# The second feed-forward's partial outputs: from sums in SBUF by DVE to copies by ACT and accumulating DMAs into DRAM

## The chip, the cores and the metric

One core of one Trainium2 chip runs the whole program. The metric is the device time of one execution in microseconds (us); the kernel before takes 995.15 us, the median of 3 runs (994.6 to 995.23).

## The reference

An attention with a memory term makes `x` of 2304 tokens by 512. Two feed-forwards follow, each with a hidden width of 2048:

```python
x = attn_out.transpose(0, 2, 1, 3).reshape(2304, 512)
h = x @ w_in                       # 512 -> 2048
x = (h * tanh(softplus(h))) @ w_out    # first feed-forward, 2048 -> 512
h = x @ w_in2
return (h * sigmoid(h)) @ w_out2       # second feed-forward
```

Inputs and output are float32.

## The kernel before, in words

The attention runs in the first 250 us. The two feed-forwards (`ph` 0 and 1) follow in 32 visits. The hidden width is cut into `NG` = 4 groups (`g`), the tokens into 4 blocks (`tp`) of 512, 640, 512 and 640 tokens. One visit `v` computes one group for one block, and the list says in which order the visits stand:

```python
VISITS = [(ph, g, tp) for ph in range(2) for g in range(NG)
          for tp in (range(4) if (g + ph) % 2 == 0 else range(3, -1, -1))]
```

So the blocks of the second feed-forward are passed as 3, 2, 1, 0, then 0, 1, 2, 3, and so on; where a group ends, the next one begins with the same block (visits 19 and 20, 23 and 24, 27 and 28). Each visit has two halves of seven products (`product`, a scheme that saves multiplications; tiles `psX`, `psW`, `psY` in PSUM, lines 962 to 964), whose results ACT and DVE turn into the hidden values `g` (lines 991 to 1003). Then `out_part` (L1030) multiplies `g` by the second weights into a PSUM tile `acc`, of which there are three. In the second feed-forward such a tile is 128 tokens by 512 outputs, and a visit has 4 or 5 of them (`d`). Every `acc` takes 12 matmuls, six from either half of the visit, and is then drained (`drain`).

A group gives only a part of the output, so four drains add up to one output tile. Before the change the sum stands in `xT` in SBUF: the first group's `acc` is copied there by ACT (L1049), the three later ones are added to it by DVE (L1051). After the last group `store` (L1056) sends the tile to the output in DRAM from SP's queue. The last tile of a block of 640 tokens (`d` = 4) lies in `xT` as four pieces of 128 elements for each partition, not as one of 512.

The order on every engine is worked out ahead of the build by a planner (`Steps.plan`): each step has an engine (P, A, D, G, S for TensorE, ACT, DVE, POOL, SP), an assumed duration, the steps that it waits for, a due time and the buffers that it holds, and a table `SHIFT` moves due times. Engines run their lists in order. SP's queue also carries the loads of the weights (L755, L759), the spills of the split inputs of a block (L940) and their reloads (L944). POOL works in the attention and for the first weights, and has nothing to do after 223 us.

Of the kernel before, what the change touches and what calls it, by code (L numbers as in the profile page):

```python
# [22 lines left out]
ALU = mybir.AluOpType  # L23
# [9 lines left out]
def latency(a, b):  # L33
    return LAT.get(a + b, 0.25)


class Steps:
# [35 lines left out]
    def plan(self):  # L73
# [15 lines left out]
        for k in reversed(topo):  # L89
            e, d, _, _, due = ops[k]  # L90
# [31 lines left out]
        while done < len(ops):  # L122
            while soon and soon[0][0] <= now + 1e-9:
                _, n, k = heapq.heappop(soon)
                heapq.heappush(ready[ops[k][0]], (late[k], n, k))
            while rel and rel[0][0] <= now + 1e-9:
                used[heapq.heappop(rel)[1]] -= 1
            moved = False
            for e in engs:
                if free[e] > now + 1e-9 or not ready[e]:  # L130
                    continue
                put_back = []
                while ready[e]:
                    it = heapq.heappop(ready[e])
                    k = it[2]
                    need = [h for h in self.takes.get(k, []) if h not in held]
                    count = {}
                    for h in need:
                        count[h[0]] = count.get(h[0], 0) + 1
                    ok = all(used[r] + c <= self.cap[r] for r, c in count.items())  # L140
                    ok = ok and all(h not in self.order_of or nexts[h[0]][0] == h for h in need)
                    if not ok:
                        put_back.append(it)
                        if len(put_back) > 40:
                            break
                        continue
                    for h in need:
                        held.add(h)
                        used[h[0]] += 1
                        if h in self.order_of:  # L150
                            nexts[h[0]].pop(0)
                    d = ops[k][1]
                    if e == "P" and self.mode.get(k, 0) != mode:
                        mode = self.mode.get(k, 0)
                        d += 0.15
                    if k in self.cols:
                        cycles, count = self.cols[k]
                        if passed.get(int(now / TICK) - 1, 0.0) < BUSY:
                            d = max(d, cycles / 1200.0)
                        t = now  # L160
                        while t < now + d - 1e-9:
                            q = int(t / TICK + 1e-9)
                            b = min(now + d, (q + 1) * TICK)
                            passed[q] = passed.get(q, 0.0) + count * (b - t) / d
                            t = b
                    self.start[k] = now
                    order.append(k)
                    free[e] = now + d
                    done += 1
                    for u in users.get(k, []):  # L170
                        left[u] -= 1
                        at[u] = max(at[u], now + d + self.lag[k] + latency(e, ops[u][0]))
                        if left[u] == 0:
                            heapq.heappush(soon, (at[u], num[u], u))
                    for h in back.get(k, []):
                        due_back[h] -= 1
                        if due_back[h] == 0:
                            heapq.heappush(rel, (now + d + 0.2, h[0]))
                    moved = True
                    break  # L180
                for it in put_back:
                    heapq.heappush(ready[e], it)
            if not moved:
                t = [x for x in free.values() if x > now + 1e-9]
                if soon:
                    t.append(soon[0][0])
                if rel:
                    t.append(rel[0][0])
                t = [x for x in t if x > now + 1e-9]
                if not t:  # L190
                    raise RuntimeError(f"stuck at {now}: " + str({e: sorted(v)[:3] for e, v in ready.items()}))
                now = min(t)
# [11 lines left out]
B, H, S, D = 4, 8, 576, 64  # L204
# [134 lines left out]
class Attn:  # L339
# [329 lines left out]
    def register(self, m):  # L669
# [6 lines left out]
        for p in range(B * NP):  # L676
# [22 lines left out]
KC = DM // P  # L699
NF = FF // P  # L700
NG = 4
# [6 lines left out]
VISITS = [(ph, g, tp) for ph in range(2) for g in range(NG)  # L708
          for tp in (range(4) if (g + ph) % 2 == 0 else range(3, -1, -1))]
# [14 lines left out]
def cuts(v):  # L724
    return [DM] if VISITS[v][0] or TBS[VISITS[v][2]] * 2 == DM else [TBS[VISITS[v][2]]]


def ps2(n):
    return 0.126 + n / 960


def sb1(n):
    return 0.093 + n / 1200
# [154 lines left out]
class Moe:  # L888
# [154 lines left out]
    def drain(self, v, d):  # L1043
        nc = self.nc
        ph, g, tp = VISITS[v]
        part, acc = self.part(v, d), self.acc.pop((v, d))
        acc = acc[:, :cuts(v)[0]] if ph == 0 else acc if d < KC else acc.rearrange("p (c n) -> p c n", c=KC)
        if g == 0:
            nc.scalar.copy(part, acc)  # L1049
        else:  # L1050
            nc.vector.tensor_tensor(part, acc, part, op=ALU.add)  # L1051

    def store(self, v, d):
        r = START[VISITS[v][2]] + d * P
        to = self.out[r:r + P, :]
        self.nc.sync.dma_start(to if d < KC else to.rearrange("p (c n) -> p c n", c=KC), self.part(v, d))  # L1056

    def register(self, m, base, ends):
        V = len(VISITS)
# [4 lines left out]
        O = lambda v, d, c: ("O", (v, c), d)  # L1064
# [3 lines left out]
        t, due, begin = base, {}, {}  # L1068
        waiting = []
        for v in range(V + 1):  # L1070
            for c in range(2):
# [3 lines left out]
                for n in seq + [0] * (len(waiting) if c or v == V else 0):  # L1075
# [3 lines left out]
                    elif waiting:  # L1079
                        k, d = waiting.pop(0)  # L1080
# [67 lines left out]
        for v, (ph, g, tp) in enumerate(VISITS):  # L1148
            w = TBS[tp]
            for c in range(2):  # L1150
# [24 lines left out]
                n = 2 * v + c  # L1175
# [7 lines left out]
            split = [("X", (comp, "comp", ph, tp), "l" + x) for x in XOPS if x[0] == "T"]  # L1183
            for d in outs(v):
                for c in range(2):
                    deps = [Q(v, c, "l0"), Q(v, c, "l1")] + [("W", (ph, g * GC + 2 * c + j, 1), "lo") for j in range(2)]
                    deps += [O(v, d, 0)] if c else ["open1"]
                    m.add(O(v, d, c), "P", od(v), deps, lambda v=v, d=d, c=c: self.out_part(v, d, c), due[O(v, d, c)],
                          cols=(6 * cuts(v)[0], 6 * cuts(v)[0]))
                    for j in range(2):  # L1190
                        last2.setdefault((ph, g * GC + 2 * c + j), []).append(O(v, d, c))
                k = ("D", v, d)
                dp = [O(v, d, 1)]
                dp += split if g == 0 else [("D", VISITS.index((ph, g - 1, tp)), d)]
                n = cuts(v)[0]
                m.add(k, "D" if g else "A", ps2(n) if g else sb1(n), dp, lambda v=v, d=d: self.drain(v, d),
                      due[O(v, d, 1)] + 1.5)
                m.hold("M.y", (v, d), [O(v, d, 0)], [k], order=(v, outs(v).index(d)))
                if ph == 1 and g == NG - 1:
                    m.add(("st", v, d), "S", 0.9, [k], lambda v=v, d=d: self.store(v, d), due[O(v, d, 1)] + 4, lag=1.5)  # L1200

        wdue = {}
        for ph, i, part in JOBS:
            g, c = i // GC, i % GC // 2
            v = next(n for n, x in enumerate(VISITS) if x[:2] == (ph, g))
# [204 lines left out]
```

## Time and profile before

| | before |
|---|---|
| median of 3 runs | 995.15 us |
| the profiled execution: its own time, its span | 995.68 us, 993.9 us |
| busy: TensorE, DVE, ACT, POOL | 954.2, 689.0, 536.5, 176.4 us |
| last matmul ends, span ends | 989.4 us, 993.9 us |
| stores of the output (L1056) | 18 of 256 KB, 915.4 to 990.2 us |

The busy times count each engine by itself; they overlap. The span runs from the first to the last instruction in the trace, and the execution's own time is 1.8 us longer. The matmul row of TensorE has modelled ends, so its busy time says that matmuls followed each other without a pause, not that each was as short as it can be.

### The profile page before, as it was taken

What the parts mean: (1) busy time and instruction counts of PE and PEld (TensorE: products, weight loads), DVE (VectorE), ACT (ScalarE), POOL (GpSimd) and SP (SyncE); (2) the same over time, 40 slices, a digit from 0 to 9 for tenths busy, and PEclk for the clock granted to TensorE, in tenths of its full rate; (3) what the DMA queues carried; (4) which work ended last, traced back from release to release, by engine and by line L of the source; (5) the groups of instructions that cost most, each with busy time, mean ns of one, the idle gap of its engine ahead of it and who ended that gap; (6) DMA issues with size and microseconds to landing.
All of it is one profiled execution on the core that took longest, in us unless ns stands there. A gap on an engine that the chain in (4) does not pass through costs nothing.

```text
span 993.9 us, 16267 instructions
## 1 busy us (share of the span) xinstructions
PE 954.2 (96%) x6080; PEld 830.0 (84%) x6080; DVE 689.0 (69%) x1584; ACT 536.5 (54%) x1215; POOL 176.4 (18%) x209
## 2 busy tenths in 40 slices
PE   6888889979999999999999999999999999999998
PEld 4555555558999999999999999998898988889986
DVE  5988899889668554974486689965664766474333
ACT  6899788878656424343343365645533543343331
POOL 4789798770000000000000000000000000000000
PEclk9999999999999999999999999999999999999999
DMA  6444243234852570165046463650472065104712
GB/s 202 131 139 124 93 146 101 95 118 195 313 183 72 196 258 1 48 235 203 19 144 220 184 247 136 240 170 1 166 251 86 22 238 204 42 1 162 235 53 75
DMA packets 56318, 142.88 MB, mean 144 GB/s; under 512 B 5040, under 2 KB 23472, under 8 KB 56240
## 3 DMA queue, kind: packets, MB, share of 16 engines
q1 hardware_dynamic: 56096, 141.52, 41.4%
q8 instruction: 48, 0.79, 0.3%
q10 hardware_dynamic: 144, 0.33, 0.1%
q14 instruction: 30, 0.25, 0.1%
HBM read 104.08 MB, written 37.75 MB: 143 GB/s over the span
## 4 chain that ended last, share of the span: by engine, by line
PE 82%; POOL 6%; DVE 5%; ACT 3%; issue 2%; DMA 1%; POOLq 0%; SPq 0%; DVEq 0%; ACTq 0%
PE acc L1030 40%; PE psX L962 7%; PE psX L963 7%; PE psX L964 7%; POOL P L583 5%; PE psY L964 3%; PE psY L963 3%; PE psY L962 3%; PE ps_t L621 2%; PE ps_s L545 2%; DVE sm L538 2%; PE psW L964 2%; PE psW L963 2%; PE psW L962 2%; PE ps_x L657 1%
## 5 line engine op out<-in xcount | busy, mean ns | idle before, releaser
L1030 PE MATMUL acc<-g,w 128*128 128x320 f32 (+1 forms) x1152 | 224.1, 337 | 0.0
L1030 PE MATMUL acc<-w,g 128*128 128x512 f32 x864 | 217.1, 394 | 0.0
L1030 PEld LDWEIGHTS acc<-g,w 128*128 128x128 f32 x1152 | 184.3, 188 | 12.4
L993 ACT COPY vt<-psX 128x256 f32<-128x256 f32 (+1 forms) x192 | 76.3, 398 | 202.1 <-PE psX L964 200.5
L1030 PEld LDWEIGHTS acc<-w,g 128*128 128x128 f32 x864 | 156.6, 188 | 29.2
L1003 DVE TENSOR_TENSOR g<-vt,g 128x640 fp32r<-128x640 f32 (+1 forms) x128 | 95.9, 753 | 71.8 <-ACT g L1002 71.6
L1051 DVE TENSOR_TENSOR xT<-acc,xT 128x512 f32<-128x512 f32 (+1 forms) x126 | 77.0, 612 | 82.8 <-PE acc L1030 82.0
L991 DVE TENSOR_TENSOR vt<-psY,vt 128x320 f32<-128x320 f32 (+1 forms) x128 | 58.1, 455 | 76.7 <-PE psY L964 45.2
L583 POOL TENSOR_SCALAR P<-P,z,g 128x448 f32<-128x448 f32 (+3 forms) x128 | 101.8, 808 | 33.4 <-DVE c L511 12.6
L568 ACT ACTIVATE P<-sm,m 128x576 f32<-128x576 f32 (+4 forms) x144 | 83.3, 581 | 14.6 <-DVE m L538 14.3
L1002 ACT CAST g<-vt 128x640 fp32r<-128x640 f32 (+1 forms) x128 | 85.5, 673 | 4.4 <-PE acc L1030 1.3
L621 PE MATMUL ps_t<-ident,P 128*128 128x128 f32 x384 | 56.9, 290 | 19.9 <-POOL P L583 18.9
L962 PE MATMUL psX<-x,w 128*128 128x256 f32 (+1 forms) x256 | 75.9, 297 | 0.0
L963 PE MATMUL psX<-x,w 128*128 128x256 f32 (+1 forms) x256 | 75.8, 296 | 0.0
L964 PE MATMUL psX<-x,w 128*128 128x256 f32 (+1 forms) x256 | 75.7, 296 | 0.0
L621 PEld LDWEIGHTS ps_t<-ident,P 128*128 128x128 f32 x384 | 43.4, 145 | 38.6 <-POOL P L583 32.3
L545 PE MATMUL ps_s<-kT,qT 64*128 64x288 f32 (+3 forms) x320 | 65.6, 495 | 7.4 <-DMA qT<-in_qT_dram 7.3
L999 ACT ACTIVATE vt<-vt 128x512 f32<-128x512 f32 (+1 forms) x64 | 43.8, 685 | 48.7 <-DVE vt L991 48.7
L998 ACT ACTIVATE vt<-psX 128x256 f32<-128x256 f32 (+1 forms) x64 | 26.3, 411 | 71.7 <-PE psX L964 71.6
L538 DVE CUSTOM_DVE_ANT_0 sm<-ps_s,mask 128x288 f32<-128x288 f32 (+3 forms) x128 | 56.6, 472 | 6.1 <-PE ps_s L545 4.6
L545 PEld LDWEIGHTS ps_s<-kT,qT 64*128 64x128 f32 x320 | 31.8, 201 | 24.6 <-issue 16.0
L962 PEld LDWEIGHTS psX<-x,w 128*128 128x128 f32 x256 | 48.5, 190 | 2.7
(110 smaller groups left out, 1999.8 us busy)
## 6 DMA issues: line engine op xcount, KB each, us to landing
stg<-in_moe_w_in_dram SPq DMA_DIRECT2D x32, 512.0 KB, 5.8
stg<-in_moe_w_out_dram SPq DMA_DIRECT2D x32, 512.0 KB, 4.1
x<-sp SPq DMA_DIRECT2D x18, 640.0 KB, 4.2
x<-sp SPq DMA_DIRECT2D x18, 512.0 KB, 4.4
sp<-x SPq DMA_DIRECT2D x12, 640.0 KB, 3.0
sp<-x SPq DMA_DIRECT2D x12, 512.0 KB, 3.4
nv<-in_v_dram SPq DMA_DIRECT2D x16, 320.0 KB, 3.0
x1T<-sp01T SPq DMA_DIRECT2D x8, 640.0 KB, 6.4
```

What stands on the lines that cost most here:

```text
L538: nc.vector.tensor_tensor_reduce(out, ps, mask, -0.125, init, ALU.add, ALU.min, acc)
L545: nc.tensor.matmul(ps, lhsT=s["qT"][R[j], qcols(i)], rhs=s["kT"][R[j], k0 + cols.start:k0 + cols.stop], start=True, stop=True)
L568: nc.scalar.activation(G(f"P{i}")[:, 1 - j if i else 1], s[f"sm{i}{j}"], AF.Exp, bias=s[f"m{i}"][:, j:j + 1], scale=-1.0, accum_out=zof(i) ...
L583: f[f"n{i}{j}"] = lambda i=i, j=j: nc.gpsimd.tensor_scalar(s[f"P{i}"][:, 1 - j], s[f"P{i}"][:, 1 - j], zof(i)[:, zcol(i, j):zcol(i, j) + 1 ...
L621: nc.tensor.transpose(ps[:, o:o + P], src, self.ident)
L962: nc.tensor.matmul(o, lhsT=W(0, kc), rhs=X(0, kc), start=(n in (1, 2, 7) and kc == 0), stop=False, skip_group_check=True)
L963: nc.tensor.matmul(o, lhsT=W(0, kc), rhs=X(1, kc), start=False, stop=False, skip_group_check=True)
L964: nc.tensor.matmul(o, lhsT=W(1, kc), rhs=X(0, kc), start=False, stop=(kc == 1), skip_group_check=True)
L1002: f[f"h{c}"] = lambda c=c: nc.scalar.copy(hi(c), val(c))
L1003: f[f"l{c}"] = lambda c=c: nc.vector.tensor_tensor(self.gt(q, c)[:, 1, :2 * tb], val(c), hi(c).bitcast(F32), op=ALU.subtract)
L1030: nc.tensor.matmul(y, lhsT=a, rhs=b, start=(c == 0 and k == 0), stop=(c == 1 and k == 5))
L1051: nc.vector.tensor_tensor(part, acc, part, op=ALU.add)
```

## The change

In the second feed-forward every partial `acc` is copied to `xT` by ACT, not added, and every partial tile is sent to the output: the first group's by a plain DMA from SP's queue, the three later groups' by DMAs from POOL's queue that add to what stands in DRAM. Such a DMA waits for the DMA of the group before on the same tile, and a copy into `xT` waits until the earlier part has been sent. The planner looks at up to 120 blocked steps (before 40) ahead of giving up.

```diff
-                        if len(put_back) > 40:
+                        if len(put_back) > 120:
...
-        if g == 0:
+        if g == 0 or ph == 1:
             nc.scalar.copy(part, acc)
         else:
             nc.vector.tensor_tensor(part, acc, part, op=ALU.add)
...
-        self.nc.sync.dma_start(to if d < KC else to.rearrange("p (c n) -> p c n", c=KC), self.part(v, d))
+        to = to if d < KC else to.rearrange("p (c n) -> p c n", c=KC)
+        if VISITS[v][1] == 0:
+            self.nc.sync.dma_start(to, self.part(v, d))
+        else:
+            self.nc.gpsimd.dma_start(to, self.part(v, d), accum_op=ALU.add)
...
-                dp += split if g == 0 else [("D", VISITS.index((ph, g - 1, tp)), d)]
+                last = [("st" if ph else "D", VISITS.index((ph, g - 1, tp)), d)] if g else []
+                dp += last if g else split
...
+                on_act = g == 0 or ph == 1
...
-                if ph == 1 and g == NG - 1:
-                    m.add(("st", v, d), "S", 0.9, [k], lambda v=v, d=d: self.store(v, d), due[O(v, d, 1)] + 4, lag=1.5)
+                if ph == 1:
+                    m.add(("st", v, d), "G" if g else "S", 1.2 if g else 0.9, [k] + last, lambda v=v, d=d: self.store(v, d), due[O(v, d, 1)] + 4, lag=1.5)
```

The end of ACT's list before the change, in the last visit (`vt` holds the hidden values before they are split, `g` the two parts after):

```order
L1002 CAST g_10379<-vt 128x640
L993 COPY vt<-psX 128x320 x2
L998 ACTIVATE vt<-psX 128x320
L1002 CAST g_10426<-vt 128x640
L999 ACTIVATE vt<-vt 128x640
L1002 CAST g_10445<-vt 128x640
L1405 UNCONDITIONAL_BRANCH
```

The same end of ACT's list with the change:

```order
L1002 CAST g_10433<-vt 128x640
L993 COPY vt<-psX 128x320
L1049 COPY xT<-acc 128x512
L993 COPY vt<-psX 128x320
L998 ACTIVATE vt<-psX 128x320
L1002 CAST g_10480<-vt 128x640
L999 ACTIVATE vt<-vt 128x640
L1049 COPY xT<-acc 128x512
L1002 CAST g_10499<-vt 128x640
L1049 COPY xT<-acc 128x512 x4
L1049 COPY xT<-acc 128x4x128
L1411 UNCONDITIONAL_BRANCH
```

The copies of `acc` have come in between the copies of `psX`, and the last five stand after everything else; the seven L1051 that DVE runs from 970 us on are gone.

The end of POOL's list, as a difference (its last row of the attention, then the new DMAs in the order of the visits; `512x1x128` is the tile in four pieces):

```order
 L602 TENSOR_SCALAR P_2982<-P_2982,z_2960,g1s 128x128
-L1405 UNCONDITIONAL_BRANCH
-L1405 ISA
+L1060 DMA out_dram<-xT 128x512 x8
+L1060 DMA out_dram<-xT 512x1x128
+L1060 DMA out_dram<-xT 128x512 x8
+L1060 DMA out_dram<-xT 512x1x128
+L1060 DMA out_dram<-xT 128x512 x4
+L1060 DMA out_dram<-xT 512x1x128
+L1060 DMA out_dram<-xT 128x512 x8
+L1060 DMA out_dram<-xT 512x1x128
+L1060 DMA out_dram<-xT 128x512 x12
```

After three more rows (one tile in pieces, eight whole ones, one in pieces) the list ends: 54 new DMAs in all, and the very last one is a tile in pieces.

The end of SP's list, as a difference (`sp12T` and `sp13T` are spilled inputs of blocks 2 and 3):

```order
 L944 DMA x0T_3040<-sp12T_7156 128x1024
-L1056 DMA out_dram<-xT 128x512
 L944 DMA x_3204<-sp_6627 128x1280
 L944 DMA x1T_3209<-sp13T_6677 128x1280
 L944 DMA x1T_3208<-sp13T_6791 128x1280
-L1056 DMA out_dram<-xT 128x512 x2
+L944 DMA x1T_3207<-sp13T_6712 128x1280
 L944 DMA x_3206<-sp_6761 128x1280
 L944 DMA x1T_3210<-sp13T_6820 128x1280
-L1056 DMA out_dram<-xT 128x512
-L944 DMA x1T_3207<-sp13T_6712 128x1280
 L944 DMA x_3205<-sp_6657 128x1280
```

The 18 stores have left this end; SP's list now ends with the last reload, and its 18 plain stores stand in the first group of the second feed-forward. TensorE's list is that of before but for two places in the second feed-forward, where six matmuls have changed places with their neighbours.

## Rows read from the trace of the kernel before

**Rows 1.** The page: busy time of each engine, and the granted clock in 40 slices.

```profile
PE 954.2 (96%) x6080; PEld 830.0 (84%) x6080; DVE 689.0 (69%) x1584; ACT 536.5 (54%) x1215; POOL 176.4 (18%) x209
...
PEclk9999999999999999999999999999999999999999
```

**Rows 2.** Windows of 20 us: engines' busy time, granted clock, share of the DMA engines, GB/s.

```profile
700.00:720.00 20.00, 20.00 (x124) 18.16 (x123) 11.04 (x22) 11.07 (x22) 0.00 (x0) 1.00 0.57 195
...
800.00:820.00 20.00, 20.00 (x118) 17.97 (x117) 11.95 (x21) 10.03 (x19) 0.00 (x0) 1.00 0.84 295
...
960.00:980.00 20.00, 20.00 (x105) 17.51 (x104) 7.82 (x12) 6.91 (x12) 0.00 (x0) 1.00 0.14 53
```

**Rows 3.** Groups by shape, 620 us to the end: busy us, mean ns, idle before.

```profile
L1030 PE MATMUL acc<-w,g 128*128 128x512 f32 x864 | 217.1, 394 | 0.0
...
L1051 DVE TENSOR_TENSOR xT<-acc,xT 128x512 f32<-128x512 f32 x55 | 37.9, 688 | 45.6 <-PE acc L1030 45.5
...
L1049 ACT COPY xT<-acc 128x512 f32<-128x512 f32 x18 | 10.5, 585 | 10.6 <-PE acc L1030 10.6
```

**Rows 4.** The chain that ended last, from 985 us on: start, us, what.

```profile
984.83 4.60 PE acc L1030 x20
989.43 0.02 issue
989.45 0.69 DVE xT L1051
```

**Rows 5.** Timeline of 969.8 to 972.9 us: start, us, engine, line.

```profile
969.94 1.56 PE L1030 MATMUL acc<-w,g 128*128 128x512 f32 x6
970.14 0.43 ACT L993 COPY vt<-psX 128x320 f32<-128x320 f32 x1 [1.47 <-PE psX L964]
...
971.34 0.31 PE L962 MATMUL psX<-x1T,w 128*128 128x320 f32 x1
...
971.54 0.69 DVE L1051 TENSOR_TENSOR xT<-acc,xT 128x512 f32<-128x512 f32 x1 [2.01 <-PE acc L1030]
...
972.42 0.43 ACT L993 COPY vt<-psX 128x320 f32<-128x320 f32 x1 [1.86 <-PE psX L964]
```

**Rows 6.** The two last stores by themselves (L1056 from 989 us, landing included).

```profile
L1056 SPq DMA_DIRECT2D out_dram<-xT x2: 332/453/574, 988.8 to 990.2; - x2
...
DMA to landing us min/median/max: 2.0/2.3/2.6
```

**Rows 7.** Windows of the end, columns as in rows 2.

```profile
989.45:990.17 0.72, 0.00 (x0) 0.00 (x0) 0.69 (x1) 0.00 (x0) 0.00 (x0) 1.00 0.74 282
990.17:991.40 1.23, 0.00 (x0) 0.00 (x0) 0.00 (x0) 0.00 (x0) 0.00 (x0) 1.00 0.13 48
991.40:992.50 1.10, 0.00 (x0) 0.00 (x0) 0.00 (x0) 0.00 (x0) 0.00 (x0) 0.83 0.85 238
```

**Rows 8.** Loads of 256 KB from DRAM, line L462, 100 to 250 us.

```profile
L462 SPq DMA_DIRECT2D nq<-in_q_dram x5: 327/328/385, 111.8 to 166.7; - x5
...
DMA to landing us min/median/max: 2.5/2.9/3.3
```

**Rows 9.** POOL's longest instruction, from its groups: busy us, mean ns.

```profile
L508 POOL TENSOR_TENSOR u<-e,z 128x640 f32<-128x640 f32 x16 | 24.9, 1553 | 6.2 <-DVE e L506 6.2
```

**Rows 10.** DVE's sums on one tile in visits 27 and 28 (timeline).

```profile
895.46 0.69 DVE L1051 TENSOR_TENSOR xT<-acc,xT 128x512 f32<-128x512 f32 x1 [2.07 <-PE acc L1030]
...
916.89 0.69 DVE L1051 TENSOR_TENSOR xT<-acc,xT 128x512 f32<-128x512 f32 x1 [1.49 <-PE acc L1030]
```

**Rows 11.** One reload by itself (L944, 745 to 746 us).

```profile
L944 SPq DMA_DIRECT2D x<-sp x1: 423/423/423, 745.2 to 745.2; - x1
...
DMA to landing us min/median/max: 7.4/7.4/7.4
```

**Rows 12.** Timeline at 760.9 us: the first matmul that reads that reload.

```profile
760.87 0.31 PE L962 MATMUL psW<-x,w 128*128 128x320 f32 x1
```

**Rows 13.** DMA queues, 620 us to the end: packets, MB, share of 16 engines.

```profile
q1 hardware_dynamic: 19032, 48.51, 37.6%
```

More of the change, by code (lines that the diff above doesn't have):

```diff
@@ L1193, in register @@
                 dp = [O(v, d, 1)]
-                dp += split if g == 0 else [("D", VISITS.index((ph, g - 1, tp)), d)]
+                last = [("st" if ph else "D", VISITS.index((ph, g - 1, tp)), d)] if g else []
+                dp += last if g else split
                 n = cuts(v)[0]
-                m.add(k, "D" if g else "A", ps2(n) if g else sb1(n), dp, lambda v=v, d=d: self.drain(v, d),
+                on_act = g == 0 or ph == 1
+                m.add(k, "A" if on_act else "D", sb1(n) if on_act else ps2(n), dp, lambda v=v, d=d: self.drain(v, d),
                       due[O(v, d, 1)] + 1.5)
                 m.hold("M.y", (v, d), [O(v, d, 0)], [k], order=(v, outs(v).index(d)))
-                if ph == 1 and g == NG - 1:
-                    m.add(("st", v, d), "S", 0.9, [k], lambda v=v, d=d: self.store(v, d), due[O(v, d, 1)] + 4, lag=1.5)
+                if ph == 1:
+                    m.add(("st", v, d), "G" if g else "S", 1.2 if g else 0.9, [k] + last, lambda v=v, d=d: self.store(v, d), due[O(v, d, 1)] + 4, lag=1.5)
         wdue = {}
```

## The prediction

> **What bounds the kernel now.** I read the page first. TensorE is busy for 954.2 of 993.9 us, DVE and ACT for far less, and the granted clock stands at nearly full speed (2.4 GHz) throughout [rows 1]. A mean over stages could hide waits, so I read windows of the second feed-forward next: in each TensorE is busy for 20.00 of 20.00 us at a granted clock of 1.00, while DVE has 8 to 12 us of work and ACT 7 to 11, and POOL none [rows 2]. The groups by shape confirm it from the other side: the matmuls into `acc` have 0.0 us of idle time before them, while DVE's additions (L1051) and ACT's copies (L1049) spend as long waiting for those matmuls as they work [rows 3]. So nothing on ACT, DVE or a DMA sets the time in this stage; its length is the sum of the matmuls. The chain that ended last shows where that stops: matmuls to 989.43 us, one addition by DVE from 989.45 us for 0.69 us, and then the last store [rows 4]. From the last matmul to the end of the span are 4.5 us, and this is the only stretch in the stage in which a faster or slower DVE, ACT or DMA shows directly.
>
> **What the change removes.** DVE loses 54 additions: 54 x 0.688 us = 37.2 us [rows 3]. TensorE waited 0.0 us for any of them, so 53 of them give nothing back. The 54th is on the path of the end and is costed below. TensorE's own list keeps every matmul; the two places where six have changed neighbours move no work.
>
> **What it adds on ACT.** 54 copies x 0.585 us = 31.6 us [rows 3], about 2.2 us more in each 20 us; the fullest window shown would hold 13.3 us instead of 11.1 [rows 2]. What matters is who stands behind such a copy: the copies out of `psX` (L993), for which TensorE waits two products later. The timeline shows the pattern: 12 matmuls of products, then 6 into `acc` (969.94 to 971.34 us), then products again. DVE starts its addition at 971.54 us, and ACT's next `psX` copy only becomes possible at 972.42 us [rows 5]. A copy of 0.585 us begun at 971.54 us ends at 972.13 us, 0.29 us before ACT is needed. As `acc` and `psX` are filled one after the other by the same engine, this holds for most of the 54. I cost these copies at nothing; what hides them is the following product on TensorE. If that cover failed at every one of them, ACT's whole 31.6 us would be the bound.
>
> **What it adds in waits.** A copy into `xT` now waits until the part before it has been sent. Closest are the places where a group ends and the next begins with the same block. For one tile there, the sum of visit 27 ends at 896.15 us and that of visit 28 starts at 916.89 us [rows 10]: a DMA has 20.7 us for issue and landing. The last two plain stores took 2.0 and 2.6 us [rows 6], and I bound an accumulating one by 6.5 us below. So ACT does not wait, and I cost this at nothing. Were it to wait, the `psX` copies would stand behind it on ACT, and TensorE behind them.
>
> **What it moves on the queues.** SP loses the 18 stores at its end and has 18 in the first group. There they stand ahead of reloads and weights, but one issue takes about 0.33 us, and the tightest reload of the stage that I found was issued at 745.2 us, landed 7.4 us later, and was first read at 760.87 us [rows 11, 12]: 8.3 us to spare. The 54 additional DMAs also load the DMA engines. From 620 us on 48.51 MB took 37.6% of 374 us [rows 13], 2.9 us for a MB, so a plain tile of 0.26 MB takes 0.76 us of all 16 engines. If an accumulating tile takes twice that (it must also read what stands in DRAM), 54 of them take 82 us in the 290 us left from about 700 us on, 0.28 of it, on top of the 0.38 that is used. The fullest window would go from 0.84 to 1.12 [rows 2]: 2.4 us of transfers slip into the next one, under the 8.3 us of slack. No cost.
>
> **The end.** Here every step is on the path.
> - ACT's copy in place of DVE's addition: 0.585 for 0.69 us, -0.1 us [rows 3, 4].
> - The last store, from its issue to its landing, took 2.6 us (the longer of the two), 0.57 us of it SP's issue, because it is the tile in four pieces [rows 6]. Now POOL issues it, and the DMA adds. The trace has neither, so I bound both. From below: nothing added, 2.6 us. From above: POOL needs as long as for its longest instruction, 1.55 us [rows 9], 1.0 us more than SP; and the whole of what stands in DRAM is read before the write begins, 2.9 us for a load of as many bytes [rows 8]. Together 6.5 us. Nothing may be gained, since no part of the plain store goes away.
> - I take 1.0 us for POOL (a DMA in 512 pieces, which already costs SP 0.57 instead of 0.33 us, is nearer to POOL's longest instruction than to nothing) and half of the read, 1.45 us, as pieces can be written while later ones are read. That is 5.05 us, +2.4 us.
> - The two tiles before it are drained 1.37 us apart. At 1.55 us for each issue POOL would be 0.4 us late for the last one; this only goes into the upper bound.
>
> Sum: -0.1 + 2.4 = **+2.3 us**. The profiled execution took 995.68 us and would take 998.0; it lies 0.53 us above the median of the three runs, so on the median's level the forecast is **997.5 us**. The bounds are -0.1 us (995.05) and -0.1 + 3.9 + 0.4 = +4.2 us (999.3). A change below 0.2% (2.0 us, from 993.2 to 997.1 us) can't be told from none here.
>
> **The rivals.**
> 1. *Only the packets of the last store get longer*, and POOL issues like SP. In the trace these packets fill 0.85 of the 1.10 us from 991.40 us on [rows 7], 0.94 us. Doubled, the end is 0.94 - 0.1 = +0.8 us longer: 996.0 us, not slower by our measure. For it: 1.2 of the 2.6 us pass before the packets, in which little moves [rows 7], so data is the smaller part of a store. Against it: whatever reads the old value has a latency of its own before the first write. It decides where POOL's issue and the read together cost under 2.1 us. The Trainium skill speaks for this rival (Collectives: The Full Stack, section The bandwidth ceiling: the fold count and why AG ≠ RS ≠ AR): adding in the DMA costs no time for the sum itself but two source reads in place of one, which halves the rate. By that rule the estimate is the 996.0 us just given; no run here shows an accumulating DMA yet.
> 2. *ACT waits for a DMA* at the three turns of the visits. It decides from the point where issue and landing take over 20.7 us [rows 10], eight times the longest of the two stores; nine of the thirteen tiles concerned wait for accumulating DMAs. At 22 us, 1.3 us of wait for each of nine, with TensorE standing: about +12 us, 1009 us.
> 3. *The DMA engines fill up* and reloads come late. In the fullest window there are 3.2 us free; with 3.7 accumulations in it the slack of 8.3 us is used up once one takes 3.1 us of all engines, four times a plain tile. At 4 us each, 11.6 - 8.3 = 3.3 us are lost at perhaps five such places: +16 us with the longer end, 1014 us.
> 4. *Faster.* DVE's 37 us would have to be what TensorE waits for somewhere. Its idle time of 0.0 us [rows 3] speaks against it; all that can be gained is the 0.1 us of the last drain.
>
> **How the numbers follow.** Forecast (TensorE unmoved, end longer by 1.2 to 4.2 us: 996.3 to 999.3 us): 0.60. Rival 1: 0.24. Rival 2: 0.05. Rival 3: 0.09. Rival 4: 0.02. Of the forecast about 0.06 lies below 997.1 us, the lower part of its own range. So faster 0.02, same 0.24 + 0.06 = 0.30, slower 0.54 + 0.14 = 0.68. The range begins at 995.3 us, a little above the lower bound, to hold most of rival 1, and ends at 1000.5 us, above the upper bound of the sum, for a mild case of rivals 2 and 3; their strong cases and rival 4 are left out.
>
> **What would show it.** In the changed kernel's profile TensorE's idle time before the matmuls stays at 0.0 us in the whole stage, and the last matmul ends at about 989.4 us; ACT's L1049 appears 72 times from 620 us on at 0.585 us, none of them released by a DMA; POOL's issues of whole tiles take under 1.37 us; the stretch from the last matmul to the end of the span grows from 4.5 to about 6.8 us. I am wrong if the last matmul ends later by over 0.5 us (rivals 2 and 3: a copy L1049 released by a DMA, or a matmul by a reload), or if the last accumulating DMA lands less than 4 us (rival 1) or more than 6.9 us after its copy ended.

## The result

The changed kernel takes 1000.43 us (median of 4 runs, 999.89 to 1001.12), the kernel before on the same chip 995.19 us (4 runs): a ratio of 1.0052 [1.0035, 1.0070], 5.2 us slower. The profiled executions, 1000.51 and 995.68 us, lie 4.83 us apart. The forecast was slower by 2.3 us, 997.5 us, with a range of 995.3 to 1000.5 us.

The page after, with engines and queues from 620 us on beneath it (the queues in the columns of [rows 13]):

```profile
PE 953.1 (95%) x6080; PEld 830.6 (83%) x6080; DVE 656.4 (66%) x1530; ACT 567.2 (57%) x1269; POOL 226.0 (23%) x263
...
q1 hardware_dynamic: 19075, 48.65, 36.8%
q0 software_dynamic: 10080, 14.16, 27.8%
```

Against [rows 1], DVE has 32.6 us less work, ACT 30.7 and POOL 49.6 us more. (The 54 additions alone are 37.2 us by [rows 3]; other instructions of DVE ran a little longer, and busy time counts instructions that overlap once.) q0 is POOL's new queue. It takes 27.8% of 379 us of the 16 DMA engines for 54 tiles, 1.95 us for each; a plain tile takes 0.76 us by [rows 13].

The groups by shape, 620 us to the end, columns as in [rows 3]:

```profile
L1030 PE MATMUL acc<-w,g 128*128 128x512 f32 x864 | 217.1, 394 | 0.0
L1060 POOL DMA_DIRECT2D out_dram<-xT x54 | 49.0, 908 | 720.0 <-DVE g L1003 502.9 <-ACT xT L1049 213.1 <-ACT vt L993 2.4
L1049 ACT COPY xT<-acc 128x512 f32<-128x512 f32 x72 | 42.2, 587 | 58.7 <-PE acc L1030 58.5
```

The matmuls into `acc` stand as in [rows 3]: the same 394 ns, nothing idle before them. ACT's copies wait for those matmuls alone. So in the stage itself nothing was gained and nothing lost. The same matmul near the start of the second feed-forward, before and after the change:

```profile
619.60 0.31 PE L962 MATMUL psX<-x1T,w 128*128 128x320 f32 x1
```

```profile
619.96 0.31 PE L962 MATMUL psX<-x1T,w 128*128 128x320 f32 x1
```

It stands 0.36 us later, and the last matmul ends 0.36 us later too, so this shift comes from ahead of the changed stage. What is left is the end. The timeline of the changed kernel from 986 us:

```profile
985.72 4.05 PE L1030 MATMUL acc<-w,g 128*128 128x512 f32 x17
...
987.96 0.86 POOL L1060 DMA_DIRECT2D out_dram<-xT  x1 [3.32 <-ACT xT L1049]
988.45 0.59 ACT L1049 COPY xT<-acc 128x512 f32<-128x512 f32 x1 [0.78 <-PE acc L1030]
989.34 0.86 POOL L1060 DMA_DIRECT2D out_dram<-xT  x1 [0.51 <-ACT xT L1049]
989.81 0.59 ACT L1049 COPY xT<-acc 128x512 f32<-128x512 f32 x1 [0.77 <-PE acc L1030]
990.69 1.19 POOL L1060 DMA_DIRECT2D out_dram<-xT  x1 [0.50 <-ACT xT L1049]
```

The last of these DMAs by itself, and the closing instructions of POOL (duration min/median/max in ns, first and last start in us):

```profile
L1060 POOL DMA_DIRECT2D out_dram<-xT x1: 1191/1191/1191, 990.7 to 990.7; - x1
...
DMA to landing us min/median/max: 5.0/5.0/5.0
...
L1411 POOLq DRAIN  x3: 40/102/7282, 990.7 to 998.5; - x3
```

The last matmul ends at 989.77 us. The DMA lands at 995.70 us. POOL's closing drain began with that last DMA, at 990.67 us; it lasts 7.28 us, until 997.95 us, and so goes on for 2.26 us after everything has landed. The span ends at 998.73 us. From the last matmul to the end of the span that is 8.96 us, against 4.46 us before. The 4.50 us are made up of three parts, by the times of both traces:

| from | before | after | difference |
|---|---|---|---|
| last matmul's end to the issue of the last DMA | 0.76 | 0.92 | +0.16 |
| issue to landing | 2.63 | 5.01 | +2.38 |
| landing to the end of the span | 1.07 | 3.03 | +1.96 |

Windows of the end, columns as in [rows 2]:

```profile
987.96:989.34 1.38, 1.38 (x7) 1.15 (x7) 0.00 (x0) 0.59 (x1) 0.86 (x2) 1.00 0.00 0
989.34:990.69 1.35, 0.43 (x2) 0.01 (x1) 0.00 (x0) 0.59 (x1) 0.86 (x1) 1.00 1.08 156
990.69:995.35 4.66, 0.00 (x0) 0.00 (x0) 0.00 (x0) 0.00 (x0) 1.19 (x1) 0.81 1.00 124
995.35:998.70 3.35, 0.00 (x0) 0.00 (x0) 0.00 (x0) 0.00 (x0) 0.00 (x0) 0.50 0.00 0
```

From 989.34 us until the last packet, at 995.35 us, the 16 DMA engines are full (1.08 and 1.00). Before the change they moved 238 GB/s at a share of 0.85 [rows 7]; now 124 GB/s fill them. Three accumulating tiles come 1.37 us apart and need 1.95 us each, so the last one queues. The 3.35 us after the last packet move nothing.

### The profile page after: what moved, and what is told of

Same layout as the page of the kernel before. It is cut to its first block, busy times and chain, and to the rows that moved or that the text cites. A ratio compares the mean times of both kernels' runs of the same rounds, so it can differ in the third digit from the quotient of the medians.

```text
span 998.7 us, 16394 instructions
## 1 busy us (share of the span) xinstructions
PE 953.1 (95%) x6080; PEld 830.6 (83%) x6080; DVE 656.4 (66%) x1530; ACT 567.2 (57%) x1269; POOL 226.0 (23%) x263
## 4 chain that ended last, share of the span: by engine, by line
PE 76%; DVE 7%; POOL 5%; issue 5%; ACT 4%; DMA 1%; SPq 0%; POOLq 0%; DVEq 0%; ACTq 0%
PE acc L1030 37%; PE psX L962 7%; PE psX L963 7%; PE psX L964 7%; POOL P L583 4%; PE psY L964 3%; PE psY L963 3%; PE psY L962 3%; DVE sm L538 2%; ACT P L568 2%; PE ps_t L621 2%; PE psW L964 2%; PE psW L962 2%; PE psW L963 2%; PE ps_s L545 1%
## 5 line engine op out<-in xcount | busy, mean ns | idle before, releaser
L1060 POOL DMA_DIRECT2D out_dram<-xT x54 | 49.0, 908 | 720.0 <-DVE g L1003 502.9
L1049 ACT COPY xT<-acc 128x512 f32<-128x512 f32 (+1 forms) x96 | 53.7, 559 | 69.9 <-PE acc L1030 69.7
L545 PE MATMUL ps_s<-kT,qT 64*128 64x288 f32 (+3 forms) x320 | 62.8, 476 | 8.3 <-DMA qT<-in_qT_dram 8.1
L1051 DVE TENSOR_TENSOR xT<-acc,xT 128x320 f32<-128x320 f32 (+1 forms) x72 | 39.9, 555 | 35.1 <-PE acc L1030 34.4
```

What stands on the lines that cost most here:

```text
L545: nc.tensor.matmul(ps, lhsT=s["qT"][R[j], qcols(i)], rhs=s["kT"][R[j], k0 + cols.start:k0 + cols.stop], start=True, stop=True)
```

## The experiments

Theory A: the whole loss is in the end, and the 39 accumulating DMAs ahead of it cost nothing. Theory B, the rival: a part of it comes from the load that those DMAs put on ACT, POOL and the DMA engines. And within the end: is it POOL's queue, the addition in the DMA, the tile in pieces, or the closing drain?

**The change without the last block.** Block 3, the last to be computed, is summed in SBUF by DVE again and stored from SP (the planner's entries follow suit).

```diff
-        if g == 0 or ph == 1:
+        if g == 0 or ph == 1 and tp != 3:
...
-        if VISITS[v][1] == 0:
+        if VISITS[v][1] == 0 or VISITS[v][2] == 3:
```

> The 13 tiles-per-group of blocks 0 to 2 keep the change (39 accumulating DMAs); block 3, whose visit is the last, is summed in SBUF by DVE and stored by SP as before. Theory (all of the +5 us lies after the last matmul, the accumulating DMAs in the middle cost nothing): the stretch from the last matmul to the end is again 4.4 to 4.6 us and the time 995.0 to 995.8 us. Rival (the accumulating DMAs also cost time in the middle, each a little): about 39/54 of the loss stays, 998.5 to 999.2 us.

Measured: 995.03 us, ratio 1.0004 [0.9995, 1.0013]. The end is that of before again, with 4.61 us from the last matmul. Its 39 accumulating DMAs are all there; POOL's drain follows the last of them, long before the end of the program:

```profile
L1060 POOL DMA_DIRECT2D out_dram<-xT x1: 859/859/859, 977.4 to 977.4; - x1
...
DMA to landing us min/median/max: 3.9/3.9/3.9
...
L1412 POOLq DRAIN  x3: 40/102/5595, 977.3 to 993.2; - x3
```

The drain lasts from 977.33 to 982.93 us, 1.64 us longer than the landing at 981.28 us, while TensorE still works; nobody waits for it. So A holds: the stretch of 4.61 us and the time are those of theory A, and the 998.5 us or more of B are refuted. A cost in the middle of up to 0.13% (1.3 us) would lie within the interval, but TensorE shows none: from the 2001st of the 6080 matmuls, in the first feed-forward, to the end of the last one pass 664.93 to 664.95 us in the profiled executions of the kernel before, the changed one and all eleven variants. Where the last matmul ends (987.4 to 989.8 us) is settled ahead of that, and so a part of the spread of the times has nothing to do with the end; the stretch after the last matmul is the sharper measure.

**Plain stores from POOL, late and early.** The kernel before, with the last five stores, or the four of visit 28, issued by POOL. The edit of the first (in the second it is `- 4`; here and below the planner's entry names POOL for the same stores):

```diff
-        self.nc.sync.dma_start(to if d < KC else to.rearrange("p (c n) -> p c n", c=KC), self.part(v, d))
+        eng = self.nc.gpsimd if v == len(VISITS) - 1 else self.nc.sync
+        eng.dma_start(to if d < KC else to.rearrange("p (c n) -> p c n", c=KC), self.part(v, d))
```

> The kernel before with only the five plain stores of the last visit issued from POOL instead of SP. Theory A (POOL's issue and POOL's own closing wait make half of the loss, the addition in the DMA the other half): issue 1.2 instead of 0.57 us, a start 0.3 us later, and POOL's drain 1.7 us after the landing: +2.4 to +3.0 us, 997.6 to 998.2 us, landing about 3.5 us after the issue. Rival B (the closing wait belongs to accumulating DMAs): +0.7 to +1.2 us, 996 to 996.4 us. Rival C (all of it is the addition): 995.0 to 995.5 us.

> The kernel before with the four plain stores of visit 28 (915 to 931 us) issued from POOL, all others from SP. Theory (POOL's closing wait follows the landing of its last DMA, so an early one is over before the end): 995.0 to 995.5 us. Rival (a fixed price at the end for every program that has used POOL's queue): +1.7 us, 996.7 to 997.2 us.

Measured: 994.97 us, ratio 1.0005 [0.9996, 1.0014], and 994.3 us, 0.9999 [0.9991, 1.0008]. The last store of the first of them, and its drain, then the drain of the second:

```profile
L1057 POOL DMA_DIRECT2D out_dram<-xT x1: 721/721/721, 989.2 to 989.2; - x1
...
DMA to landing us min/median/max: 2.7/2.7/2.7
...
L1406 POOLq DRAIN  x3: 40/93/2952, 989.2 to 992.9; - x3
```

```profile
L1406 POOLq DRAIN  x3: 40/93/6445, 929.2 to 991.5; - x3
```

A plain store of the tile in pieces lands 2.67 us after POOL's issue, as after SP's (2.63 us), though the issue itself is longer (0.72 for 0.57 us). POOL starts it 0.29 us after DVE's result, SP 0.03 us. A whole tile lands 2.28 us or more after POOL's issue and 2.00 after SP's. The drain ends 0.26 us after the landing; in the second kernel it ends at 935.66 us, 0.21 us after the landing at 935.45 us, long before the program's end. The stretch of the first is 4.94 us, so a few plain stores from POOL cost about 0.5 us at the end, and none earlier. Theory A and rival B were too high. Rival C's number came out, but its reason, that all of the loss is the addition, does not hold (see No addition). For the early stores the fixed price of the rival is refuted.

**The order of the last tiles.** In the last visit the tile in pieces is computed first, in the changed kernel and in the one before:

```diff
-            VISITS[v][0] == 0) else list(range(2 * TBS[VISITS[v][2]] // P))
+            VISITS[v][0] == 0) else [4, 0, 1, 2, 3] if v == V - 1 else list(range(2 * TBS[VISITS[v][2]] // P))
```

> The changed kernel with the tile in four pieces taken first in the last visit, so that the very last DMA is a whole tile. Theory (POOL's issue is 0.86 instead of 1.19 us and its pieces of 2 KB pass faster than 512 B ones): 0.6 to 1.5 us less than the changed kernel, 998.9 to 999.8 us, landing 4.0 to 4.4 us after the issue. Rival (the queue of three accumulating tiles behind each other sets the landing): at most the 0.3 us of the issue less, 1000.1 us.

> The kernel before with the tile in four pieces taken first in the last visit, so that the last store, plain and from SP, is a whole tile: SP's issue 0.33 instead of 0.57 us and landing 2.0 instead of 2.6 us after it. Theory: stretch 3.9 instead of 4.5 us, a gain of 0.6 us, 993.9 to 994.6 us, under what a comparison of times can show but to be read in the trace. Rival (the landing is set by latency, not by the pieces): no change in the stretch.

Measured: 999.1 us, ratio 1.0046 [1.0032, 1.0060], and 994.43 us, ratio 0.9994 [0.9985, 1.0003]. The last DMA of the changed kernel with this order:

```profile
L1060 POOL DMA_DIRECT2D out_dram<-xT x1: 859/859/859, 988.4 to 988.4; - x1
...
DMA to landing us min/median/max: 5.6/5.6/5.6
...
L1411 POOLq DRAIN  x3: 40/102/7831, 988.4 to 996.8; - x3
```

POOL's issue is 0.33 us shorter, yet the DMA lands 5.55 us after it, not 5.01 us. Ahead of it stand two whole accumulating tiles, as in the changed kernel; the tile in pieces had landed at 984.60 us, before any of these three was issued. So the pieces are not what makes the end long; the queue of accumulating tiles sets the landing, as the rival said, and the theory's 4.0 to 4.4 us were missed. Why three whole tiles take 0.5 us longer is not shown. The time lies in the theory's range by luck: the stretch after the last matmul is 9.51 us, longer than the changed kernel's 8.96, and the last matmul ended 2.3 us earlier. In the kernel before the same order does shorten the end, from 4.46 to 3.86 us, as the theory said (the last store lands 2.04 us after its issue, not 2.63); its gain in time is too small to tell from none.

**No addition.** The changed kernel with 54 plain DMAs from POOL:

```diff
-            self.nc.gpsimd.dma_start(to, self.part(v, d), accum_op=ALU.add)
+            self.nc.gpsimd.dma_start(to, self.part(v, d))
```

> The changed kernel with all 54 DMAs of POOL plain; nothing is added, so the output holds the last group's part alone. Theory (the addition is the price: it keeps the DMA engines about 2 us for each tile, and POOL's drain ends 2.2 us after the landing only behind accumulating DMAs): the stretch from the last matmul to the end falls from 8.9 to about 4.9 us as with five plain DMAs from POOL, 994.5 to 995.5 us; the last lands 2.6 to 2.8 us after its issue, the drain ends 0.3 us after that. Rival (54 DMAs from POOL cost at the end by their number, whatever they do): the drain stays 2.2 us behind, 997 to 997.5 us.

Measured: 996.96 us, ratio 1.0018 [1.0010, 1.0027]: 1.8 of the 5.2 us remain.

```profile
L1060 POOL DMA_DIRECT2D out_dram<-xT x1: 717/717/717, 989.7 to 989.7; - x1
...
DMA to landing us min/median/max: 2.7/2.7/2.7
...
L1411 POOLq DRAIN  x3: 40/102/5226, 989.7 to 995.4; - x3
```

Its queue of POOL from 620 us on, in the columns of [rows 13], with 379 us as the whole:

```profile
q0 software_dynamic: 4320, 14.16, 9.9%
```

That is 0.70 us of all 16 engines for a tile, against 1.95 us with the addition, 2.8 times as much for the same 54 tiles. The landing is back at 2.68 us, as the theory said. The drain is not: it ends 2.52 us after the landing, where five plain stores had 0.26 us. Here the rival was right, and the theory's 994.5 to 995.5 us were missed. So the two large parts of the loss are separate: the addition makes the landing late, and the drain is long without it.

**One, five and eighteen accumulating DMAs at the end of the kernel before.** The edit of the second of them; the first has `and d == 4` in the condition, the third has no condition:

```diff
-        self.nc.sync.dma_start(to if d < KC else to.rearrange("p (c n) -> p c n", c=KC), self.part(v, d))
+        to = to if d < KC else to.rearrange("p (c n) -> p c n", c=KC)
+        if v == len(VISITS) - 1:
+            self.nc.gpsimd.dma_start(to, self.part(v, d), accum_op=ALU.add)
+        else:
+            self.nc.sync.dma_start(to, self.part(v, d))
```

> The kernel before with only the very last store an accumulating DMA from POOL, all others plain from SP; it adds to what the output held before the run. Theory (the late landing in the changed kernel is a queue of tiles that come 1.37 us apart and take about 2 us each): alone it lands 3.5 to 4.2 us after its issue instead of 5.0, and the drain follows 2.2 us after the landing: stretch about 7.5 us, 997.0 to 998.0 us. Rival 1 (no queue, one tile takes 5.0 us): 8.9 us, 998.5 to 999.5 us. Rival 2 (the drain grows with the number of accumulating DMAs behind it): 0.3 to 0.6 us for one, stretch 5.9 us, 995.5 to 996.3 us.

> The kernel before with the five stores of the last visit accumulating DMAs from POOL, the other 13 plain from SP; they add to what the output held before the run. Theory (queue of the last three tiles and the drain, nothing from the 49 earlier ones): the same end as the changed kernel, landing 5 us after the last issue, drain 2.2 us later, stretch 8.9 us, 998.5 to 999.5 us. Rival (the number of accumulating DMAs in the whole program counts): a drain of under 1 us, 997 to 998 us.

> The kernel before, but all 18 stores of the output's tiles (not only the last five) are accumulating DMAs from POOL; they add to whatever stands in the output, so the output is not the reference's. Theory (count): after the last DMA has landed, POOL's closing drain goes on for about 0.043 us for each DMA that POOL issued in the program, whatever kind they are. The runs so far: 0.09 us after 1, 0.26 after 5, 1.64 after 39, 2.26 to 2.52 after 54. For 18 that gives 0.8 us (0.7 to 0.9), a stretch from the last matmul to the end of the span of 8.4 us (7.9 with five), and a time 4.1 us above before's. Rival (place): the drain is long only where many DMAs are in the middle of the program, over several groups of visits; then 0.3 us as with five, a stretch of 7.9 us and a time 3.6 us above before's.

Measured: 997.38 us, ratio 1.0022 [1.0013, 1.0032]; 998.62 us, 1.0035 [1.0022, 1.0048]; 999.46 us, 1.0045 [1.0028, 1.0062]. With one, the DMA engines are idle when it comes, and two windows show what an accumulating DMA takes by itself:

```profile
990.55:992.00 1.45, 0.00 (x0) 0.00 (x0) 0.00 (x0) 0.00 (x0) 1.38 (x1) 0.93 0.00 0
992.00:994.47 2.47, 0.00 (x0) 0.00 (x0) 0.00 (x0) 0.00 (x0) 0.00 (x0) 0.50 0.94 106
```

POOL's issue takes 1.38 us (the program's first DMA from POOL, which takes some 0.2 us more than later ones: 1.10 us for 0.86 us in the changed kernel), in which nothing moves; then the packets of the tile in pieces fill 0.94 of 2.47 us, 2.3 us of all 16 engines, where the plain one took 0.94 us [rows 7]. It lands 4.25 us after the issue. With the two whole tiles before it also accumulating it lands 5.63 us (five) and 5.91 us (eighteen) after it, so there is a queue, and rival 1 of the first run is refuted. The drains, in the same order:

```profile
L1409 POOLq DRAIN  x3: 40/93/4362, 990.5 to 995.5; - x3
```

```profile
L1409 POOLq DRAIN  x3: 40/93/5910, 989.5 to 996.2; - x3
```

```profile
L1406 POOLq DRAIN  x3: 40/102/6722, 988.8 to 996.0; - x3
```

They end 0.09, 0.26 and 0.79 us after the last landing. The five here and the five plain ones have the same 0.26 us, though they make 1104 and 400 packets: neither the kind nor the packets set it, the number of DMAs does. Nor is it the number of rows that the DMAs write: one tile in pieces and the four whole tiles of visit 28 are 512 rows each, and have 0.09 and 0.21 us. For eighteen the count theory had said 0.8 us, the rival 0.3.

The times of one and of five lie in the ranges of their theories by luck. Both theories had a drain of 2.2 us after the landing, and in both runs the rival with the count is the one nearer to the drain. The stretches are 6.63 us (one; the theory said 7.5) and 7.90 us (five; 8.9). Eighteen have 8.51 us, for the 8.4 of the count theory; their time, 4.9 us above before's by the medians, is 0.8 us more than it said, with runs from 998.0 to 999.9 us.

**More, smaller DMAs.** The changed kernel without the addition, each transfer in two halves (108 DMAs), or only those of the second and third group (90). The edit of the second; the first cuts all of them in two:

```diff
-            self.nc.gpsimd.dma_start(to, self.part(v, d), accum_op=ALU.add)
+            part = self.part(v, d)
+            h = part.shape[1] // (1 if VISITS[v][1] == NG - 1 else 2)
+            for at in range(0, part.shape[1], h):
+                self.nc.gpsimd.dma_start(to[:, at:at + h], part[:, at:at + h])
```

> The changed kernel without the addition in the DMA, and each of POOL's 54 transfers sent as two of half the columns, so 108 plain DMAs of half the size; partial outputs overwrite each other, the output is not the reference's. Theory (count): the closing drain goes on for 108 x 0.043 to 0.047 = 4.6 to 5.1 us after the last landing (2.5 with 54), the stretch from the last matmul to the end grows from 6.9 to about 9.7 us (0.5 us of it a second issue before the last landing), and the time is 4 to 5 us above before's. Rival (bytes or engines: the drain goes by what was moved): 2.5 us after the landing as with 54, a stretch of about 7.4 us, and a time 2 to 2.5 us above before's.

> The changed kernel without the addition in the DMA, and the transfers of the second and third group of visits sent in two halves each, those of the last group whole: 90 plain DMAs from POOL instead of 54 or 108; the output is not the reference's. With 108 the closing drain went on for only 0.50 us after the last landing, but POOL stood for 2.67 us ahead of its 105th issue, waiting for nothing that the profile shows. Theory (a list that POOL clears: each DMA that it issued leaves about 0.045 us of work, done in the closing drain, or at once when the list is full, at a number between 90 and 104): no pause ahead of an issue here, and the drain goes on for 90 x 0.043 to 0.047 = 3.9 to 4.2 us after the last landing; the stretch from the last matmul to the end is 8.5 us (6.9 with 54) and the time 3.3 to 3.8 us above before's. Rival (the drain's length has a limit, near the 2.5 us of the 54, and the pause with 108 was something else): 2.2 to 2.7 us after the landing, a stretch of 6.9 us, a time 1.8 us above before's.

Measured: 997.75 us, ratio 1.0027 [1.0015, 1.0039], with 108, and 1000.34 us, 1.0059 [1.0042, 1.0075], with 90. The drain with 90, and then POOL's last DMAs with 108 (timeline):

```profile
L1414 POOLq DRAIN  x3: 40/102/8166, 989.1 to 997.7; - x3
```

```profile
988.51 0.54 POOL L1063 DMA_DIRECT2D out_dram<-xT  x1
989.83 0.59 ACT L1049 COPY xT<-acc 128x512 f32<-128x512 f32 x1 [0.77 <-PE acc L1030]
991.73 0.56 POOL L1062 DMA_DIRECT2D out_dram<-xT  x1 [2.67 <-issue]
992.27 0.54 POOL L1063 DMA_DIRECT2D out_dram<-xT  x1
992.81 0.72 POOL L1062 DMA_DIRECT2D out_dram<-xT  x1
993.51 0.73 POOL L1063 DMA_DIRECT2D out_dram<-xT  x1
```

With 90 plain DMAs the drain goes on for 5.45 us after the landing and the kernel is 6.0 us slower than before, without one addition in a DMA and with the bytes of the 54. For 90 both expectations were missed: the rival's limit of 2.7 us is refuted, and the count theory's 3.9 to 4.2 us are too little. With 108 POOL stands for 2.67 us ahead of its 105th issue, waiting for nothing that the trace names, and the drain after the landing is then only 0.50 us; neither theory had that, though the time, 3.2 us above before's by the medians, lies between them. That most of the work behind the earlier DMAs was done in that pause would fit; no run isolates it.

| DMAs from POOL | kind | drain's end after last landing, us | for each, ns |
|---|---|---|---|
| 1, 5, 18 | accumulating | 0.09, 0.26, 0.79 | 90, 52, 44 |
| 4 (visit 28), 5 | plain | 0.21, 0.26 | 52, 52 |
| 39 (the change without the last block) | accumulating | 1.64 | 42 |
| 54 (the change) | accumulating | 2.26 | 42 |
| 54 | plain | 2.52 | 47 |
| 90 | plain, most of half size | 5.45 | 61 |
| 108 | plain, half size | 0.50, and 2.67 of pause | |

## Why the prediction was right in its direction and too small

**TensorE is not moved: right.** No idle time before the matmuls into `acc`, the last matmul 0.36 us later than before, under the 0.5 us named as the limit, and these 0.36 us are there before the second feed-forward begins. The change without the last block shows it from the other side: 39 accumulating DMAs in the middle change the time by nothing that can be measured.

**DVE's relief is worth nothing, ACT's copies are hidden, no copy waits for a DMA: right.** 72 copies at 587 ns, none released by a DMA, though one of the 54 DMAs took 9.2 us to land; at the turns of the visits there were 20.7 us [rows 10]. Rival 2 did not occur.

**The DMA engines: an accumulating tile costs more than assumed, and it mattered in another place.** I assumed 1.5 us of all engines, twice a plain tile; measured are 1.95 us, 2.6 times my 0.76 us and 2.8 times the 0.70 us of the same tiles without the addition. In the stage the slack of the reloads took it, as forecast (rival 3 did not occur). In the end I let the last tile wait for POOL's issue alone, of the three tiles that come 1.37 us apart. POOL's 0.86 us was no limit; the engines' 1.95 us was.

**Issue to landing: the sum was right, its parts were not.** Predicted 5.05 us, measured 5.01 us. But the 1.0 us that I put on POOL's issue are 0.62 us (1.19 for 0.57 us), and the other 1.45 us, put down to half a read of the old value, are 1.76 us of longer packets and of a queue. One accumulating DMA into idle engines landed 2.87 us after POOL's issue had ended, that of the changed kernel 3.81 us: the queue adds 0.9 us. The two errors cancelled.

**The step that failed is the list of the end's steps: it stopped at the landing.** I took the 1.07 us from the landing to the end of the span as fixed. They became 3.03 us: POOL's closing drain goes on for 2.26 us after the landing. These 1.96 us, and the 0.27 us by which POOL starts later than SP after its input is ready, are all that separates the measured stretch (8.96 us) from the predicted 6.8 us. In the kernel before POOL issues no DMA, and its drain ends with POOL's own work, before 224 us; no row of that trace shows what a drain does after DMAs. That the drain depends on the number of POOL's DMAs is shown from 1 to 90. With 54 plain DMAs the drain and POOL's later start alone cost 1.8 us of time, and the addition accounts for the rest of the loss.

**That the time fell inside the range is luck.** 1000.43 us lie above the sum's own upper bound (999.3 us). They are 0.07 us under the end of the range, which was put there for mild cases of rivals 2 and 3, and neither occurred.

**Rival 1, that only packets get longer, was refuted with its price.** It was to show in a landing less than 4 us after the last copy's end; measured are 5.3 us (990.40 to 995.70 us). The Trainium skill (Collectives: The Full Stack, section The bandwidth ceiling: the fold count and why AG ≠ RS ≠ AR) has two source reads for one where a collective's reduce step adds in the DMA. This case agrees in the direction: for the tile in pieces 2.3 us of the 16 engines for 0.94 us, a factor of 2.5. Longer packets are one part of the loss beside POOL's issue, the queue and the drain.

Of the 5.2 us by medians, the end accounts for 4.50 us of the profiled pair and the last matmul's place, which the change did not cause, for 0.36 us; the other 0.4 us lie within the spread of the runs (1.2 to 1.6 us).

**What stays open.** Why the drain lasts as long as it does. Up to 54 DMAs 42 to 52 ns each fit (a single one 90), but from 54 to 90 plain ones it grows by 2.92 us, 81 ns each, and with 108 a part seems to move into a pause. Work of some 40 ns for each DMA that is done once during the flight of the last one and once more after its landing would fit both slopes; this was worked out afterwards and not tried. The 18 to 54 accumulating ones, of which the change consists, lie on the line.

No run was faster than the kernel before by an amount that can be measured. The change without its last block equals it, with 39 x 0.69 = 27 us of DVE's work moved and nothing gained from it.

## What to carry to other kernels

When an engine's queue gets its first DMAs, look at what that engine does at the end of the program: the closing drain of POOL grew with the number of DMAs that it had issued, and it is hidden only if the last of them is issued well before the program ends. Keep the last stores on the queue and in the form that land fastest, and do sums that accumulate in DRAM where TensorE still has work. An accumulating DMA is priced by the engines' time that its packets take (here 2.8 plain tiles), and tiles that arrive faster than that queue up; relief for an engine that nobody waits for pays none of it back.

## What was not expected of the hardware

- POOL's closing drain: 7.28 us long in the changed kernel, 2.26 us past the last landing, and up to 5.45 us past it with 90 plain DMAs.
- POOL's issues: 0.54 us for a whole plain tile and 0.72 us for one in pieces; 0.86 and 1.19 us with the addition; the first issue of a program is some 0.2 us longer. A plain tile in pieces lands about as soon after POOL's issue as after SP's (2.67 and 2.63 us), a whole one a little later (2.28 and 2.00 us at the least).
- POOL stood for 2.67 us ahead of the 105th of 108 DMAs; with 90 there was no such pause.
